# Output transposes by DMA for half of the batches, a merged scaling of k, a third pair buffer and a new schedule model in an attention and mixture-of-experts kernel

## The chip, the cores and the metric

The kernel runs on one core of one Trainium2 chip. The metric is the device time of one execution in microseconds. A program is executed several times; the text gives the median of the runs and, where the scatter matters, every run. Where two kernels are compared by a ratio, it is the mean time of the fast runs of one over the mean of the fast runs of the kernel before that ran in the same rounds on the same chip. It is therefore not quite the ratio of the medians that stand beside it. A ratio comes with its 95% interval.

## The reference

There are two parts, one behind the other. The first is an attention with a feature map ("hedgehog"), without a softmax over positions: 8 batches, 8 heads, 576 positions of 64 numbers. The second is a mixture of 8 experts over the 4608 rows that come out, with a routing table made by 8 rounds of alternate row and column scaling.

```python
def phi(x):                                   # x: batch, head, 576, 64
    proj = einsum('bhsd,df->bhsf', x, w_phi)  # 64 -> 128
    proj = proj - max(abs(proj), axis=-1)
    return concatenate([exp(proj), exp(-proj)], axis=-1)

q_p, k_p = phi(q), phi(k)
kv  = einsum('bhsf,bhsd->bhfd', k_p, v);  z = sum(k_p, axis=2)
x   = einsum('bhsf,bhfd->bhsd', q_p, kv) / (einsum('bhsf,bhf->bhs', q_p, z) + 1e-06)
# x is put into 4608 rows of 512

P = exp(x @ w_gate - max)                     # 4608 x 8
for _ in range(8):                            # routing
    P /= P.sum(1) + 1e-09;  P /= P.sum(0) + 1e-09;  P *= N / E
for e in range(8):
    out += P[:, e] * (relu(x @ w1[e]) @ w2[e])
```

## The kernel before

The work goes through the core as follows.

- **Attention**, to about 212 us. Two heads of a batch make a *pair*; there are 32 of them. For most batches the inputs q and k of two pairs are loaded as 16-bit numbers (tile `qk`) and turned by a DMA transpose on the SyncE queue (`qkT<-qk`, 12 of them, 512 KB each). TensorE multiplies them with `wphi`, VectorE takes maxima (`m`), ScalarE takes exponentials (`k`, `q`, `em`), GpSimd scales v, and the output of a pair (`xb`) is turned again into `xT`, the operand of the experts.
- **Expert 0** is computed plainly. TensorE is not busy with attention alone, so the expert's matmuls fill its gaps. Its weights come in eight pieces (`load_w0`).
- **Routing**, from about 214 to 257 us: a chain of small VectorE operations and one tiny matmul (`cs` by `colw`) in each of 8 rounds, again with expert 0's matmuls as filling.
- **Experts 1 to 7**, each with a scheme of seven products in place of eight, from about 263 us to the end.

Every operation is first recorded with its engine, its estimated duration and its dependencies. A list scheduler then plays the kernel through with those durations and gives each engine a fixed order. The chip executes that order: **each engine does its instructions in the planned sequence, and if the first one must wait, those behind it wait too.** The queue of SyncE goes by its order too: in the kernel before it waited once 14.7 us for GpSimd with a load, and the transfers behind were issued after that, the next of them at 36.7 us. Which operation is preferred is set by the string `order`, each letter of which starts one step of a pair.

```python
class Plan:                                   # parts of schedule()
    ...
    free[o.eng] = at + o.dur
    ...
    if o.nbytes:                              # a DMA: one line for all of them
        dma_free = max(at + o.dur + 1.0, dma_free) + o.nbytes / 1e3
        o.end = dma_free + 1.0
    else:
        o.end = at + o.dur + o.lat
...
def load_w(e, r=()):                          # weights of experts 1 to 7, 2 MB of HBM data in each DMA
    for w, src in ((w1, moe_w1), (w2, moe_w2)):
        dma("POOL", 2 << 20, 280, ... nc.gpsimd.dma_start(out=w(), in_=src[e]...), r, ...)
...
def load_w0(i, r):                            # expert 0: pieces 0-3 are w1, 4-7 are w2
    n = i % 4
    if i < 4:
        dma("POOL", 1 << 19, 250, ... out=w1()[:, :, n * 256:(n + 1) * 256] ..., r, [(w1, n)])
    else:
        dma("POOL", 1 << 19, 280, ... out=w2()[:, 2 * n:2 * n + 2, :] ..., r, [(w2, n)])
...
# pair_a: both signs of k
mk = scores(1, 1)
for y, sg in ((0, -1.0), (1, 1.0)):
    em = s["em"][y]
    exp(10, lambda em=em: em(), lambda: m()[:, 1, :], sg, mk, [em])
    pool(512, lambda ...: nc.gpsimd.tensor_tensor(out=s["v"][y]()[:, :, 0:D], in0=t["v"]()..., in1=em()..., op=ALU.mult), ...)
    pool(4, lambda ...: nc.gpsimd.tensor_copy(out=s["v"][y]()[:, :, D], in_=em()), ...)
...
def pair_c(b, pr, xb):
    if b < 8:                                 # always
        pxt = new("P1")
        for j in range(NJ):
            pe(128, lambda j=j: nc.tensor.transpose(bf(pxt)[:, j * 128:j * 128 + 128], xb()[:, j, :], ident), ...)
        dve(256, lambda: nc.vector.tensor_copy(out=xT[:, pr, b * SM:(b + 1) * SM], in_=bf(pxt)[:, 0:512]), ...)
    else:
        ...                                   # a DMA transpose on the SyncE queue, never taken
...
def stage_a(i):                               # pair i = 4 b + pr
    ...
    gt = [("max", 0, i - 1)] if i >= 1 else []
    if b + 1 < B and pr in (0, 2):            # loads for the next batch
        ...
        load_qk(b + 1, 2 * pr, 4, t, gt); load_v(...); turn_qk(t)
    ...
    n = i - 2
    if 0 <= n < 8:
        load_w0(n, gt)                        # one piece of expert 0 with each pair from the third
...
def sums_x(g):                                # sums of parts of x for the seven products
    X = [new("S") for _ in range(2)]
    for n, y, z, r in (...):
        sub(dve, 512, x(n), y, z, ALU.subtract, xkeys(g) + ["late"] + ..., ...)
    for i in range(2):
        dma("SP", 1 << 18, 250, lambda i=i: nc.sync.dma_start(out=Xd[g][i], in_=X[i]()), ...)
...
if e == 1 and g < 9:                          # the 36 scalings of expert 0's result
    for ts in range(4):
        act(512, lambda ts=ts: nc.scalar.activation(out=acc[g][:, ts, :], in_=acc[g][:, ts, :],
            func=ACT.Copy, bias=0.0, scale=P[:, 4 * g + ts, 0:1]), ["P", ("acc", g, ts)] + akey(g), ...)
...
for e in range(1, E):
    w1, w2 = load_w(e, [("xT", 5, 3)])        # "late" would be: after all of attention
    if e == 1:
        for g in range(NG):
            sums_x(g)
```

## Time and profile before

The kernel before took 1044.54 us (three runs, 1044.49 to 1044.91). In the four later batches of runs its medians were 1044.8 to 1045.0, single runs 1043.5 to 1047.0.

The table by stretches gives, for each stretch of time, the busy time of each engine, the granted clock of TensorE (1.00 is full), the mean number of DMA transfers' packets in work as a share of the engines, and GB/s. These are three of its rows for the kernel before, with the row of column names:

```profile
core 0: us, PE busy (x) PEld busy (x) DVE busy (x) ACT busy (x) POOL busy (x), PEclk, DMA share, GB/s
...
20.00:70.00 50.00, 44.01 (x508) 28.82 (x506) 46.79 (x116) 46.56 (x121) 37.91 (x73) 1.00 1.15 181
...
262.00:300.00 38.00, 35.24 (x304) 29.25 (x303) 26.70 (x47) 37.28 (x74) 10.99 (x9) 1.00 0.34 72
300.00:1040.00 740.00, 739.01 (x6738) 658.93 (x6735) 565.11 (x1008) 458.16 (x958) 314.64 (x250) 1.00 0.27 69
```

TensorE is busy for 739.01 of the 740 us from 300 to 1040 us, so there is no more than about 1 us of gaps to fill there. From 20 to 70 and from 262 to 300 us there is more, 6.0 and 2.8 us. The ends of matmuls are modelled in the profile, so a busy share is a rough number. I therefore also took the step from each matmul's start to the next one's start and compared it with the step of a full stream. For N columns I set that to N/2.4 + 2.5 ns, an estimate: a line through the median steps of this trace, which are 0.056 us between matmuls of 128 columns, 0.109 us for 256 and 0.216 us for 512 (0.160 us more for 384 columns more). What a step takes beyond that is a *stall* if it is over 2.5 times this floor, otherwise it is counted as *slow clock*. The name says more than the trace does: in every stretch of the kernel before the granted clock is 1.00, so for its slow steps a lower clock is not shown. This is a computation of mine from the trace.

Who was waited for from 20 to 70 us shows in the view of waits. Its columns are the engine and line that waited, the operation waited for, and the total, the count and the longest of these waits in us. TensorE in the kernel before:

```profile
engine line waited for: us in total, times, longest us
PE P L407 <- DVE m L399: 2.0, 7, 0.7
PE P L606 <- DVE P L618: 0.8, 2, 0.5
PE P L484 <- DVE m L399: 0.6, 1, 0.6
```

All waits are short ones, and all are for VectorE or ScalarE. No wait for a DMA is in the list. For 255 to 300 us the chain of work that ended last tells what sets the time, in shares of the stretch. Its summary line for the kernel before:

```profile
by line: ACT acc L1181 36.2%; ACT V L1171 13.9%; ACT U L1047 13.8%; issue 8.2%; ACT hT L1056 7.2%; PE P L1019 6.6%; PE P L407 4.4%; DVE hT L1051 3.1%; ACT acc L734 2.1%; DVE acc L1159 1.8%; DVE T L927 1.4%; DVE P L886 1.0%; DVE c_bc L884 0.
```

L1181 is the scaling of expert 0's result, 36 operations on ScalarE. They all become possible at once when the routing ends, and stand in ScalarE's way while it should empty PSUM for expert 1. The groups of instructions that the change touches, up to 345 us (columns: line, engine, operation, tiles and shapes, count | busy us, mean ns of one | idle time before, and for whom):

```profile
L626 DVE TENSOR_TENSOR xb<-P,rec 128x256 bf16<-128x256 f32 x64 | 26.9, 421 | 1.0
...
L1181 ACT ACTIVATE acc<-acc,P 128x512 f32<-128x512 f32 x36 | 25.0, 782 | 0.8 <-DVE P L886 0.8
...
L648 DVE COPY xT<-P 128x512 bf16<-128x512 bf16 x32 | 13.3, 416 | 1.2 <-PE P L645 1.1
...
L645 PE MATMUL P<-ident,xb 128*128 128x128 bf16 x128 | 12.9, 219 | 0.3 <-DVE m L399 0.2
...
L403 ACT ACTIVATE em<-m 128x8 f32<-128x8 f32 x64 | 10.7, 236 | 0.5 <-DVE m L399 0.4
...
L631 DVE TENSOR_TENSOR xb_r<-P,rec 128x128 bf16<-128x128 f32 x32 | 9.0, 281 | 0.0
```

### The profile page before, as it was taken

What the parts mean: (1) busy time and instruction counts of PE and PEld (TensorE: products, weight loads), DVE (VectorE), ACT (ScalarE), POOL (GpSimd) and SP (SyncE); (2) the same over time, 40 slices, a digit from 0 to 9 for tenths busy, and PEclk for the clock granted to TensorE, in tenths of its full rate; (3) what the DMA queues carried; (4) which work ended last, traced back from release to release, by engine and by line L of the source; (5) the groups of instructions that cost most, each with busy time, mean ns of one, the idle gap of its engine ahead of it and who ended that gap; (6) DMA issues with size and microseconds to landing.
All of it is one profiled execution on the core that took longest, in us unless ns stands there. A gap on an engine that the chain in (4) does not pass through costs nothing.

```text
span 1043.5 us, 24529 instructions
## 1 busy us (share of the span) xinstructions
PE 1020.4 (98%) x9512; PEld 842.1 (81%) x9512; DVE 823.9 (79%) x1626; ACT 711.1 (68%) x1570; POOL 461.5 (44%) x532
## 2 busy tenths in 40 slices
PE   6899999999999999999999999999999999999998
PEld 4566666654788888888888888888888888888886
DVE  6999899998777787778877787778777877787775
ACT  7999999944976666666666666565666666666663
POOL 3876757500233344344444444444444443333442
PEclk9999999999999999999999999999999999999999
DMA  9997987734411152113311441134111611114333
GB/s 250 150 196 132 150 127 136 122 122 120 93 41 41 52 105 60 51 42 82 81 41 42 87 87 51 42 69 95 41 42 50 125 51 42 41 43 131 122 122 122
DMA packets 105237, 93.94 MB, mean 90 GB/s; under 512 B 45344, under 2 KB 80288, under 8 KB 105120
## 3 DMA queue, kind: packets, MB, share of 16 engines
q1 hardware_dynamic: 71840, 68.45, 23.6%
q0 software_dynamic: 33120, 23.86, 16.4%
q8 instruction: 74, 1.21, 0.5%
q14 instruction: 43, 0.35, 0.1%
q10 hardware_dynamic: 160, 0.07, 0.0%
HBM read 94.98 MB, written 14.16 MB: 105 GB/s over the span
## 4 chain that ended last, share of the span: by engine, by line
PE 89%; ACT 5%; DVE 3%; DMA 1%; issue 1%; SPq 0%; POOL 0%; DVEq 0%; ACTq 0%
PE P L1019 70%; PE P L407 16%; ACT acc L1181 2%; DVE m L399 1%; PE P L606 1%; ACT k L403 1%; DMA acc<-in_q_dram 1%; DMA wgate_f<-in_moe_w_gate_dram 1%; ACT V L1171 1%; ACT U L1047 1%; PE P L645 1%; DVE xb L626 0%; ACT q L403 0%; DVE P L618 0%; PE P L484 0%
## 5 line engine op out<-in xcount | busy, mean ns | idle before, releaser
L1174 POOL TENSOR_TENSOR acc<-acc,V 128x512 f32<-128x512 f32 x248 | 316.4, 1283 | 440.4 <-ACT V L1171 437.2
L1051 DVE CUSTOM_DVE_ANT_0 hT<-P,U 128x512 bf16<-128x512 f32 x378 | 255.0, 687 | 107.9 <-ACT U L1047 59.7
L1047 ACT COPY U<-P 128x512 f32<-128x512 f32 x378 | 217.8, 590 | 137.4 <-PE P L1019 130.8
L1171 ACT ACTIVATE V<-P,P 128x256 f32<-128x256 f32 x496 | 206.3, 477 | 123.4 <-PE P L1019 121.6
L1159 DVE SCALAR_TENSOR_TENSOR acc<-P,P,acc 128x256 f32<-128x256 f32 x372 | 160.1, 478 | 73.4 <-PE P L1019 71.7
L1019 PEld LDWEIGHTS <-w 128*128 128x128 bf16 x2016 | 197.3, 98 | 23.7 <-issue 0.6
L1019 PEld LDWEIGHTS <-S 128*128 128x128 bf16 x1984 | 194.1, 98 | 23.2 <-issue 0.6
L1019 PEld LDWEIGHTS <-T 128*128 128x128 bf16 x1512 | 147.9, 98 | 19.1 <-issue 2.0
L1019 PEld LDWEIGHTS <-hT 128*128 128x128 bf16 x1488 | 145.4, 98 | 18.3 <-DVE hT L1051 1.1
L1019 PE MATMUL P<-X,w 128*128 128x256 bf16 x1008 | 154.7, 273 | 0.4 <-ACT U L1047 0.4
L1019 PE MATMUL P<-xT,w 128*128 128x256 bf16 x1008 | 152.0, 273 | 0.0
L1019 PE MATMUL P<-X,T 128*128 128x256 bf16 x1008 | 148.6, 273 | 1.3 <-ACT U L1047 1.2
L1019 PE MATMUL P<-w,hT 128*128 128x256 bf16 x992 | 142.6, 273 | 0.6 <-DVE hT L1051 0.6
L1019 PE MATMUL P<-T,S 128*128 128x256 bf16 x1056 | 136.3, 273 | 0.4 <-ACT V L1171 0.4
L1019 PE MATMUL P<-w,S 128*128 128x256 bf16 x928 | 126.6, 273 | 0.0
L532 POOL TENSOR_TENSOR v<-v_m,em 128x512 bf16<-128x512 f32 x64 | 66.8, 1043 | 70.6 <-ACT em L403 57.5
L399 DVE TENSOR_REDUCE m<-P 128x4 f32<-128x512 f32 x128 | 82.7, 681 | 1.7 <-PE P L407 1.2
L1056 ACT ACTIVATE hT<-P 128x512 bf16<-128x512 f32 x126 | 74.6, 607 | 12.9 <-PE P L1019 12.4
L407 PE MATMUL P<-w,hT 128*128 128x512 bf16 x320 | 80.2, 379 | 0.3
L927 DVE TENSOR_TENSOR S<-hT 128x1024 bf16<-128x1024 bf16 x124 | 80.1, 683 | 0.0
L407 PE MATMUL P<-xT,w 128*128 128x512 bf16 x288 | 76.2, 379 | 1.2 <-ACT kr L403 0.5
L1019 PE MATMUL P<-xT,T 128*128 128x256 bf16 x504 | 76.3, 273 | 0.0
(94 smaller groups left out, 1091.7 us busy)
## 6 DMA issues: line engine op xcount, KB each, us to landing
X<-xd SPq DMA_DIRECT2D x126, 256.0 KB, 2.6
w<-in_moe_w_dram POOLq DMA_DIRECT2D x14, 1024.0 KB, 10.4
v_m<-in_v_dram SPq DMA_DIRECT2D x15, 512.0 KB, 5.1
out_dram<-acc SPq DMA_DIRECT2D x14, 512.0 KB, 3.2
xd<-S SPq DMA_DIRECT2D x18, 256.0 KB, 2.0
qk<-in_k_dram POOLq DMA_DIRECT2D x12, 256.0 KB, 5.5
qk<-in_q_dram POOLq DMA_DIRECT2D x12, 256.0 KB, 6.4
w<-in_moe_w_dram POOLq DMA_DIRECT2D x8, 256.0 KB, 7.5
```

What stands on the lines that cost most here:

```text
L399: dve(el, lambda: nc.vector.tensor_reduce(out=dst(), in_=src(), axis=AX.X, op=ALU.max, apply_absolute_value=True), r, w)
L407: nc.tensor.matmul(out_, lhsT=lhsT, rhs=rhs, start=start, stop=stop)
L532: pool(512, lambda y=y, em=em: nc.gpsimd.tensor_tensor(out=s["v"][y]()[:, :, 0:D], in0=t["v"]()[:, h0:h0 + 2].rearrange("p a (b c) -> p (a ...
L927: lambda: f.tensor_tensor(out=out_(), in0=x(), in1=y(), op=op), r, w, **kw)
L1019: pe(256, lambda i=i, k=k, z=z: nc.tensor.matmul(bank()[:, 256 * i:256 * i + 256], lhsT=lhs(k, i), rhs=rhs(k), start=first and z, stop=k = ...
L1047: act(512, lambda: nc.scalar.copy(out=u[fp][n]().rearrange("p a b -> p (a b)"), in_=x[fp]()), [x[fp]], [u[fp][n]])
L1051: dve(500, lambda: nc.vector._custom_dve(ADD_SAT, out=out_(fp, i, j), in0=bank[fp]().rearrange("p (a b) -> p a b", a=2), in1=u[fp][n](), s ...
L1056: act(512, lambda: nc.scalar.activation(out=out_(fp, i, j), in_=x[fp]().rearrange("p (a b) -> p a b", a=2), func=ACT.Relu, bias=0.0, scale ...
L1159: dve(330, lambda n=n, ts=ts: nc.vector.scalar_tensor_tensor(out=acc[g][:, ts, 256 * j:256 * j + 256], in0=bank()[:, 256 * n:256 * n + 256 ...
L1171: act(390, lambda n=n: nc.scalar.activation(out=u()[:, n, :], in_=bank()[:, 256 * n:256 * n + 256], func=ACT.Copy, bias=0.0, scale=P[:, 4 ...
L1174: pool(670, lambda: nc.gpsimd.tensor_tensor(out=acc[g][:, 2 * i:2 * i + 2, 256 * j:256 * j + 256], in0=acc[g][:, 2 * i:2 * i + 2, 256 * j: ...
L1181: act(512, lambda ts=ts: nc.scalar.activation(out=acc[g][:, ts, :], in_=acc[g][:, ts, :], func=ACT.Copy, bias=0.0, scale=P[:, 4 * g + ts, ...
```

## The change

Its intent is to take work off TensorE, VectorE and ScalarE in attention, and to order the rest better:

1. The outputs of batches 3 to 6 (16 pairs) are turned by DMA transposes on the SyncE queue instead of TensorE transposes and VectorE copies.
2. Both signs of the scaling of k are done in one operation: GpSimd writes the negative maxima beside the maxima, one exponential serves both, and one GpSimd multiplication of 1024 elements replaces two of 512.
3. The output of a pair is made in steps of five columns each (with the rest rows inside), so `xb` takes two VectorE operations in place of three.
4. The pair's buffers get a third copy. Its room is taken from the second weight buffer (`wx`), so the weights of expert 1 can't be loaded before attention has ended.
5. The schedule model gets DMA landing times, for which it takes two queues to share the links, a TensorE clock that it can take to be slower, and new speeds and durations. These are assumptions of the model. The order string is new and has finer steps.
6. The 36 scalings wait for the second `hT` of their group, so they spread over expert 1.

The core of the diff:

```diff
@@ schedule model
+class Links:
+    def add(self, o, at):
+        n = int(o.eng == "POOL")
+        self.line[n].append([at + (2.6 if n else 1.65), o.nbytes / 1e3, o])
...
+        share = [1.0, 1.0]
+        if len(on) == 2:
+            share = [0.23, 0.59] if self.line[0][0][2].turn else [0.59, 0.42]
...
-                dma_free = max(at + o.dur + 1.0, dma_free) + o.nbytes / 1e3
-                o.end = dma_free + 1.0
+                links.add(o, at)          # lands at the time of Links, + 0.95
@@ rings
-    ring(wp, [128, 4, FF], BF16, "w1", 2)
-    ring(wp, [128, 8, DD], BF16, "w2", 2)
+    wx = wp.tile([128, 8192], BF16, name="wx")
+    ring(wp, [128, 4, FF], BF16, "w1", 1, 1)      # the second copy is a view of wx
+    ring(wp, [128, 8, DD], BF16, "w2", 1, 1)
-        ring(a_t, [128, 8, DF], BF16, f"k{x}", 2)
+        ring(a_t, [128, 8, DF], BF16, f"k{x}", 2, 1)
...
@@ pair_a
-        for y, sg in ((0, -1.0), (1, 1.0)):
-            em = s["em"][y]
-            exp(10, lambda em=em: em(), lambda: m()[:, 1, :], sg, mk, [em])
-            pool(512, ...)
+        pool(8, lambda: nc.gpsimd.tensor_scalar_mul(m()[:, 1], m()[:, 2], -1.0), mk, [(m, "neg")])
+        exp(16, lambda: em(), lambda: m()[:, 1:3], 1.0, mk + [(m, "neg")], [em])
+        pool(1024, ...)
@@ outs
-            if h == 0:
-                dve(128, lambda: nc.vector.tensor_tensor(out=r["xb"]()[:, pr]..., 
+            dve(320, lambda: nc.vector.tensor_tensor(
+                out=xb()[:, :, 64 * h:64 * h + 64], in0=num()[:, :, 0:D], ...
@@ pair_c
-        if b < 8:
+        if b in (3, 4, 5, 6,):
+            dma("SP", 1 << 17, 148, lambda: nc.sync.dma_start_transpose(
+                out=xT[:, pr, b * SM:(b + 1) * SM]..., in_=xb()[:, 0:NJ]...), ...)
+            return
@@ order
-        "aqraqabbcqabqacbqrbcaqbacuqaqbacqruabgqccucbudbduaqabdqadgrcbucqucabqcauqdua" ...
+        "arqparqbabqbapqnbaqamqmbnpabqpnpbmnpccnrcnpamqcaqpmbupaqumcacrnbqnuanbqampun" ...
@@ scaling of expert 0
-                    scale=P[:, 4 * g + ts, 0:1]), ["P", ("acc", g, ts)] + akey(g),
+                    scale=P[:, 4 * g + ts, 0:1]), ["P", ("acc", g, ts), (hT[1], 0, 1)] + akey(g),
@@ experts
-        w1, w2 = load_w(e, [("xT", 5, 3)])
+        w1, w2 = load_w(e, ["late"])
```

## The prediction

> **What bounds it now.** TensorE. From 300 us on, the table by stretches gives 20.0 busy of every 20 us, with 128x256 matmuls starting 0.109 us apart. [...] I took the step from each matmul's start to the next in TensorE's timeline and compared it with that floor: only 23.6 us are stalls, against about 1,011 us of work; 3.7 us pass before the first matmul and about 6 us after the last. The stalls: 5.1 us before 20 us (start-up, waiting for the first q, k transfers), 11.2 us from 20 to 70, none from 70 to 140, 3.1 us from 140 to 212, none from there to 260, and 4.2 us from 260 to 300. So attention looks bound by ScalarE and VectorE (46.6 and 46.8 busy of 50 us from 20 to 70), but only where TensorE has no expert-0 matmuls to fill with.
>
> **What the change does.**
> - TensorE: 64 output transposes (16 pairs) go to the DMA queue. At 0.055 us a step that is 3.5 us; splitting the rest-row matmuls adds about 0.3. Net -3.2 us, nearly all on the critical path, as it lies in a saturated stretch.
> - VectorE: 16 evictions of 0.416 us go (-6.7 us); the three xb operations of a pair (421+421+281 ns) become two of 320 elements, about 491 ns each by interpolation: -4.5 us in all.
> - ScalarE: 64 em operations of 236 ns and 16 em_r of 227 ns halve: -9.3 us. GpSimd gets a negation per pair, and one 1024-element multiply for two of 1.04 us: a longer chain (about 1 us, an estimate from these) to v, which the third pair buffer should cover.
> - DMA: 16 more transposes of 128 KB on the SyncE queue. The existing ones of 512 KB take 5.3 us to land; DMA engines are 70-90% busy in attention, yet TensorE waited for DMA only at start-up.
> - Expert 1's weights now load after attention (first at 178 us before); landing takes 10-15 us and they are needed at about 257, so no wait.
> - The 36 scalings of acc (782 ns, 25 us of ScalarE between 257 and 300, 36% of that stretch's chain) must now wait for their group's hT, so they spread over expert 1.
>
> **How much shows.** From 70 to 260 savings on ScalarE and VectorE mostly hide. I count: -3.2 TensorE work; 20-70 us: 5% less ScalarE work and better packing, -3.5; 140-212: -1.5; 260-300: -3. Start-up and the rest: nothing, or a little lost to new DMA waits. Together about -11 to -12 us.
>
> **Prediction: 1032.5 us, range 1026.5 to 1039.** Faster by over 2% needs under 1023.6, practically all stalls gone: 4%. Within 2%: 95%. Slower by over 2%: 1%.
>
> **What would show it.** Right: output transposes on TensorE from 128 to 64; steps over the floor fall in 20-70 and 260-300; the first expert-1 matmul comes at about 253 instead of 263; ScalarE and VectorE together lose about 20 us in attention; from 300 us on the stretches stay at 20.0, the last matmul simply earlier. Wrong: TensorE waiting for xT or acc from DMA, for expert-1's w near 250, or for v from GpSimd.
>
> **What would make it wrong.** A late first expert-0 matmul (the new order starts it after nine pairs begun, before after seven)[...]; transposes blocking input loads behind them in the in-order SyncE queue; the longer GpSimd chain. On the other side, the new order may nearly empty 20-70.

Two passages are cut from this text. The first took the floor of a matmul's step from elsewhere and concluded that the part from 300 us on is at it; the floor that the text speaks of after that is the line through measured steps given above. -3.2, -3.5, -1.5 and -3 us come to -11.2 us, the text's -11 to -12.

## The result and the profile after

The changed kernel took 1041.64 us: 1043.33, 1039.95, 1038.93 and 1043.44 (ratio to before 0.997, 0.9951 to 0.9988). A second set of four, run later as a control on another occasion, gave 1040.73, 1042.53, 1036.26 and 1041.74 (0.9955, 0.9926 to 0.9985). It is a little faster, by some 3 to 4 us instead of 11 to 12, and the measured median lies above the upper end of the predicted range. It also scatters over 7 us, where the kernel before scatters over 3.5.

The profiled execution is the one of 1043.33 us. The same three rows of its table by stretches:

```profile
20.00:70.00 50.00, 41.93 (x485) 28.26 (x483) 42.92 (x102) 43.03 (x106) 36.15 (x59) 0.93 1.43 167
...
262.00:300.00 38.00, 38.00 (x332) 32.27 (x330) 27.79 (x48) 29.71 (x59) 10.94 (x9) 1.00 0.41 84
300.00:1040.00 740.00, 737.01 (x6719) 657.15 (x6716) 567.28 (x1004) 468.73 (x980) 314.61 (x250) 1.00 0.27 70
```

The last stretch but one is now full, as hoped. From 20 to 70 us TensorE is busy for 2.1 us less than before, and at a lower granted clock (0.93 instead of 1.00). The accounting of TensorE's steps by stretch, in us, stall + slow clock (differences taken before rounding):

| stretch | before | after | predicted difference | found |
|---|---|---|---|---|
| 0-20 | 5.8 + 2.3 | 2.9 + 2.7 | 0 or a small loss | -2.4 |
| 20-70 | 11.2 + 2.9 | 12.8 + 4.6 | -3.5 | +3.4 |
| 70-140 | 0.0 + 0.7 | 4.2 - 0.2 | 0 | +3.3 |
| 140-212 | 3.1 + 0.9 | 0.4 - 0.2 | -1.5 | -3.7 |
| 212-262 | 0.0 - 0.5 | 2.5 + 1.6 | 0 | +4.6 |
| 262-300 | 4.2 + 0.2 | 0.2 + 0.1 | -3 | -4.1 |
| work at full speed | 1004.2 | 1001.0 | -3.2 | -3.2 |

The gains came, and two of them were larger than predicted: 3.2 + 2.4 + 3.7 + 4.1 = 13.4 us. Against them stand three losses where none, or a gain, was predicted: 3.4 + 3.3 + 4.6 = 11.3 us. That leaves about 2 us, and by so much the last matmul starts earlier (1038.64 before, 1036.70 after).

The groups of instructions that answer to those shown before, up to 345 us, and the chain of 262 to 300 us:

```profile
L1412 ACT ACTIVATE acc<-acc,P 128x512 f32<-128x512 f32 x28 | 20.5, 736 | 0.0
...
L865 DVE TENSOR_TENSOR xb<-ps,rec 128x320 bf16<-128x320 f32 x32 | 15.3, 484 | 0.4
...
L883 DVE COPY xT<-ps 128x512 bf16<-128x512 bf16 x16 | 6.3, 410 | 0.4 <-PE ps L880 0.3
...
L564 ACT ACTIVATE em<-m 128x16 f32<-128x16 f32 x22 | 6.1, 277 | 0.5 <-POOL m L754 0.5
...
L880 PE MATMUL ps<-ident,xb 128*128 128x128 bf16 x40 | 3.9, 228 | 0.1
```

```profile
by line: PE ps L1250 91.0%; PE ps L568 9.7%; issue 0.0%
```

The edits of single operations did what they are meant to. The output copies fell from 32 to 16. The exponential `em` is one of 277 ns instead of two of 236 (22 of the 32 stand here under the tile `em`; the other 10 lie in `wx`, as do some of `xb` and of the transposes). The scalings (L1412, before L1181) are 28 in this window instead of 36, the others come later, and they are out of the chain.

**The loss from 20 to 140 us.** The waits of TensorE in the changed kernel, first from 20 to 70, then from 70 to 140 us:

```profile
PE ps L568 <- DMA qkT<-qk: 3.5, 1, 3.5
PE ps L851 <- DVE m_r L560: 1.0, 1, 1.0
```

```profile
PE ps L568 <- DMA qkT<-qk: 2.0, 2, 1.5
```

TensorE now waits for turned inputs, `qkT`, which it never did before. The chain that ended last, from 20 to 70 us, consists of them for two thirds; the first line is its summary, the others are the two pieces (start, us, what):

```profile
by line: DMA qkT<-qk 68.2%; PE ps L568 9.3%; ACT q L564 5.4%; ACT k L564 3.6%; issue 3.4%; PE ps L698 3.1%; DVE m L560 2.6%; DVE m_r L560 2.6%; ACT wx L564 1.5%; PE ps L851 1.3%; PE ps L624 1.3%; DVE ps L859 1.0%; DVE xb L865 1.0%; DVE rec 
```

```profile
36.81 17.45 DMA qkT<-qk
...
55.98 16.67 DMA qkT<-qk
```

The DMA view has the time from issue to landing. The line is of the transposes issued in the ten microseconds around the first one, once in the kernel before and once in the changed one (KB are not given for a transpose; the last number is us to landing):

```profile
qkT<-qk SPq DMA_TRANSPOSE x1, 5.6
```

```profile
qk<-in_q_dram POOLq DMA_DIRECT2D x1, 256.0 KB, 17.6
...
qkT<-qk SPq DMA_TRANSPOSE x1, 17.4
```

The transpose took 5.6 us to land before and 17.4 us after, as did the other transfers issued beside it: the next q took 17.6 us. The new order itself makes part of this crowd: by 45 us it has issued seven of expert 0's eight weight pieces, the old order three, and the eight land after 7.6 to 19.3 us instead of 4.0 to 8.8 us. TensorE's timeline shows what the wait costs twice over:

```profile
54.30 1.89 PE L568 MATMUL ps<-wphi,qkT 128*128 128x256 bf16 x8 [3.54 <-DMA qkT<-qk]
```

```profile
72.69 1.05 PE L568 MATMUL ps<-wphi,qkT 128*128 128x256 bf16 x8 [0.49 <-DMA qkT<-qk]
```

After a wait of 3.54 us the eight matmuls of 256 columns took 1.89 us, after a wait of 0.49 us 1.05 us. The granted clock (view by stretches) was 0.50 from 52.84 to 59.66 us: it fell while TensorE waited, and the next 5.4 us of matmuls ran at it. From 72.5 to 74 us it was 1.00. How long a wait must be for this is not shown: after the wait of 2.3 us at the routing (below) the clock was 0.50 from 226.92 to 230.33 us, and from 70 to 140 us, with waits for `qkT` of up to 1.5 us, it was 1.00.

How much room each turned input had is best told by its *slack*: TensorE's arrival at the first matmul that needs it, minus the landing. A negative slack is a wait. I computed it from the trace for all 12 transposes; of each, the first three as issue time, us to landing and slack:

| kernel | 1st | 2nd | 3rd | median of 12 | least |
|---|---|---|---|---|---|
| before | 43: 5.6, +5.3 | 61: 10.6, +2.2 | 70: 5.2, +9.5 | +8.7 | +1.3 |
| after | 37: 17.4, -4.0 | 56: 16.7, -0.9 | 72: 8.3, +0.9 | +1.1 | -4.0 |

A late landing is not new: one of the kernel before took 14.3 us, at 184 us, and still had 1.3 us to spare. What is new is that there is no room for one.

**The loss from 212 to 262 us.** The wait of TensorE from 212 to 300 us, and VectorE's longest from 205 to 262:

```profile
PE ps L568 <- DVE cs L1110: 2.3, 1, 2.3
```

```profile
DVE S L1158 <- DMA xd<-S: 2.5, 1, 2.5
```

`cs` is the routing's column sum. Three pieces of the chain that ended last show why it was late:

```profile
215.65 8.14 DMA xd<-S
...
223.81 0.42 DVE S L1158
...
225.84 26.05 PE ps L568 x119
```

VectorE makes the sums of x, which are stored to `xd` from a buffer with few copies. A sum must wait until an older one's store has landed, and the routing's next operation stands behind that sum in VectorE's order. The stores landed late because expert 1's weights, which had been loaded from 178 us on before, now start at 214 us. The stores issued in 205 to 235 us, and the weights beside them:

```profile
xd<-S SPq DMA_DIRECT2D x10, 256.0 KB, 2.1
```

```profile
xd<-S SPq DMA_DIRECT2D x10, 256.0 KB, 7.1
wx<-in_moe_w_dram POOLq DMA_DIRECT2D x2, 1024.0 KB, 14.7
```

### The profile page after: what moved, and what is told of

It reads as the page before. It is cut to its first block, busy times and chain, and to the rows that moved or that the text cites. A ratio compares the mean times of both kernels' runs of the same rounds, so it can differ in the third digit from the quotient of the medians.

```text
span 1041.5 us, 24345 instructions
## 1 busy us (share of the span) xinstructions
PE 1017.8 (98%) x9512; PEld 841.2 (81%) x9512; DVE 821.2 (79%) x1576; ACT 704.9 (68%) x1530; POOL 459.2 (44%) x476
## 4 chain that ended last, share of the span: by engine, by line
PE 91%; DMA 5%; ACT 1%; DVE 1%; POOL 1%; issue 0%; DVEq 0%; SPq 0%; POOLq 0%; ACTq 0%
PE ps L1250 73%; PE ps L568 15%; DMA qkT<-qk 4%; PE ps L851 1%; DMA xd<-S 1%; ACT k L564 1%; ACT q L564 0%; PE ps L698 0%; DMA xT<-xb 0%; DMA acc<-in_k_dram 0%; POOL vrd L678 0%; POOL v L756 0%; DVE S L1158 0%; DVE m L560 0%; DVE m_r L560 0%
## 5 line engine op out<-in xcount | busy, mean ns | idle before, releaser
L1278 ACT COPY U<-ps 128x512 f32<-128x512 f32 x378 | 217.1, 587 | 172.2 <-PE ps L1250 163.0
L1282 DVE CUSTOM_DVE_ANT_0 hT<-ps,U 128x512 bf16<-128x512 f32 x378 | 254.4, 686 | 82.5 <-PE ps L1250 58.0
L1402 ACT ACTIVATE V<-ps,P 128x256 f32<-128x256 f32 x496 | 208.3, 473 | 85.8 <-PE ps L1250 78.9
L1390 DVE SCALAR_TENSOR_TENSOR acc<-ps,P,acc 128x256 f32<-128x256 f32 x372 | 159.7, 477 | 78.9 <-PE ps L1250 78.6
L1250 PE MATMUL ps<-X,T 128*128 128x256 bf16 x1008 | 151.2, 273 | 0.0
L1250 PE MATMUL ps<-T,S 128*128 128x256 bf16 x1056 | 135.8, 273 | 0.1
L1250 PEld LDWEIGHTS <-wx 128*128 128x128 bf16 x1152 | 112.7, 98 | 13.6 <-issue 0.2
L1250 PEld LDWEIGHTS <-w 128*128 128x128 bf16 x864 | 84.5, 98 | 9.8
L1250 PE MATMUL ps<-xT,wx 128*128 128x256 bf16 x576 | 88.7, 273 | 0.0
L1250 PE MATMUL ps<-X,wx 128*128 128x256 bf16 x576 | 86.5, 273 | 0.0
## 6 DMA issues: line engine op xcount, KB each, us to landing
wx<-in_moe_w_dram POOLq DMA_DIRECT2D x8, 1024.0 KB, 10.2
```

What stands on the lines that cost most here:

```text
L1250: pe(256, lambda i=i, k=k, z=z: nc.tensor.matmul(bank()[:, 256 * i:256 * i + 256], lhsT=lhs(k, i), rhs=rhs(k), start=first and z, stop=k = ...
L1278: act(512, lambda: nc.scalar.copy(out=u[fp][n]().rearrange("p a b -> p (a b)"), in_=x[fp]()), [x[fp]], [u[fp][n]])
L1282: dve(515, lambda: nc.vector._custom_dve(ADD_SAT, out=out_(fp, i, j), in0=bank[fp]().rearrange("p (a b) -> p a b", a=2), in1=u[fp][n](), s ...
L1390: dve(320, lambda n=n, ts=ts: nc.vector.scalar_tensor_tensor(out=acc[g][:, ts, 256 * j:256 * j + 256], in0=bank()[:, 256 * n:256 * n + 256 ...
L1402: act(370, lambda n=n: nc.scalar.activation(out=u()[:, n, :], in_=bank()[:, 256 * n:256 * n + 256], func=ACT.Copy, bias=0.0, scale=P[:, 4 ...
```

## The experiments

**Theories.** *D (landing times)*: the new order gives DMA-fed operands hardly any slack; the turned inputs land late because expert 0's weight pieces, the next inputs and the transposes crowd the DMA engines from 30 to 60 us, and that sets the loss from 20 to 140 us. *S (stores)*: the moved load of expert 1's weights delays the stores of the sums, and that sets the loss from 212 to 262 us. *Rivals*: the 16 new output transposes on the SyncE queue hold up the input transposes behind them (T); the longer chain over GpSimd for the scaling of k costs more than it saves (G); the tighter order itself, with any slack, would lose as much elsewhere (E). The recorded expectations use other letters: their A is D, their A2 is S, their B is T. Their C is that the new order asks for the first turned input too early whatever the traffic. Their E is that deeper rings make the input loads the limit; the E of this text is wider. The cold or slow clock of which they speak is the granted clock of 0.50 from 52.84 to 59.66 and from 226.92 to 230.33 us in the changed kernel's trace; half of TensorE's busy time there, 2.7 and 1.7 us, is an estimate of what it cost.

**A measure that helps.** The schedule model holds a planned start for every operation. It is no measurement, but the trace minus the plan, the *lag*, shows exactly where an execution falls behind its own plan. For the profiled execution of the changed kernel ScalarE's lag (VectorE's agrees) is 1.3 us at 50 us, 7.3 at 70, 10.1 at 90, 10.5 at 210, 15.1 at 230 and 15.9 at the end. So nearly all of the time is lost at three places, and these are the waits above. The kernel before can't be read in this way: its own model plans an end some 70 us after the measured one, so that its lag only falls.

### 1. The moved load and the scalings by themselves

Both are edits of the kernel before. The first, the load of the weights after attention:

```diff
-        w1, w2 = load_w(e, [("xT", 5, 3)])
+        w1, w2 = load_w(e, ["late"])
```

> The kernel before with one thing of the change: weights of experts 1 to 7 may load only after attention, so expert 1's two loads issue at about 213 us instead of 178. If theory A2 holds, stores of xd land in 3 us or more in the median instead of 2.0, VectorE and then TensorE wait between 215 and 240, where the kernel before shows none, and it is 1 to 5 us slower (1045.5 to 1049.5). If the load time does not matter there: within 1 us of 1044.5.

Measured: 1043.9 us (before 1044.95 in the same rounds; ratio 0.999, 0.9975 to 1.0005). The expectation failed. The weights took 8.3 and 16.6 us and the first four stores 6.7 to 8.5 us, nearly as in the changed kernel, but VectorE did not wait for them: in the old order the sums stand where there is room. So a late load alone costs nothing. It costs time in an order that has no room for it.

The second, the scalings behind their group's `hT`:

```diff
-                    scale=P[:, 4 * g + ts, 0:1]), ["P", ("acc", g, ts)] + akey(g),
+                    scale=P[:, 4 * g + ts, 0:1]), ["P", ("acc", g, ts), (hT[1], 0, 1)] + akey(g),
```

> The kernel before with one thing of the change: each of the 36 scalings of acc by P for expert 0 waits, in the schedule, for the hT of its group. If these scalings, bunched on ScalarE after 262 us, cause TensorE's 4.2 us of stalls from 260 to 300 (prediction: -3), those stalls fall under 1 us and the kernel takes 1040 to 1041.5 us. If the stalls come from the start of expert 1 itself: still 3 us or more, time unchanged within 1 us.

Measured: 1041.54 us (0.9969, 0.9954 to 0.9984), so 3.4 us for one dependency. The stalls and slow steps from 262 to 300 us fell from 4.4 to 0.9 us. The chain from 255 to 300 us, whose largest part was `acc L1181` with 36.2%, is now:

```profile
by line: PE P L1019 79.0%; PE P L407 18.3%; DVE hT L1051 2.8%; issue 0.2%
```

This one line of the change is worth about what the whole change gained.

### 2. The output transposes by themselves

On the kernel before, half of the outputs turned by DMA, and the same together with the scalings:

```diff
-        if b < 8:
+        if b not in (3, 4, 5, 6):
             pxt = new("P1")
```

> The kernel before with one part of the change: outputs of batches 3 to 6 turned by DMA. My count: 64 transposes of 55 ns off TensorE, so TensorE's work falls by 3.5 us and the time to 1040.5 to 1042.5 if no DMA wait appears. Rival B (the output transposes delay the input transposes on the same in-order queue): landings of qkT after 100 us lengthen, their slack falls under 2 us, TensorE waits for qkT or xT, and the gain is under 1.5 us.

> The kernel before with the two parts that helped it alone: the scalings of acc gated by hT (measured -3.4 us) and outputs of batches 3 to 6 turned by DMA (-1.8 us). If independent: 1039 to 1040.5, with runs within 1.5 us of each other, as the old order has a median of 8 us between a turned input's landing and its use. If they overlap: 1041 to 1042.

Measured: 1043.07 us for the transposes alone (before 1044.86; 0.9983, 0.9968 to 0.9998), and 1041.23 us for both (before 1044.98; 0.9965, 0.995 to 0.998). The expectation for the transposes, 1040.5 to 1042.5 us, was missed by 0.6 us; why they give less than their 3.5 us of TensorE work was not looked into. The single gains of 1.8 and 3.4 us have a sum of 5.2, together they gave 3.75; each of these has an interval of some 1.5 us to either side, so this does not show that they overlap. The 16 transposes of 128 KB landed in 2.4 to 11.7 us, and no input waited for them.

On the changed kernel the outputs go back to TensorE. The model plans anew:

```diff
-        if b in (3, 4, 5, 6,):
+        if b in ():
```

> The changed kernel with all outputs turned on TensorE as in batches 0 to 2. If the output transposes by DMA are the gain that was counted: 2 to 5 us slower than the changed kernel (1043 to 1047), TensorE's work up by 3.5 us. If they are what ate the gain (rival B): faster than the changed kernel, and the waits for qkT between 36 and 100 us gone. Theory D says those waits stay, because the first output transpose is issued at 109 us.

Measured: 1047.89 us (1052.96, 1046.13, 1045.98, 1049.65), about 6 us slower than the changed kernel. Not all of it is TensorE's work: the new plan, from an order string tuned for the old one, ends 6.3 us later in the model already (1031.7 instead of 1025.5 us). The wait for the first turned input is still there, as its waits from 35 to 70 us show:

```profile
PE ps L568 <- DMA qkT<-qk: 4.2, 1, 4.2
```

So rival T falls: the output transposes, the first of which is issued at 109 us, don't cause these waits. What they are worth by themselves is told by the 1.8 us above, not by this newly planned kernel.

### 3. The crowd around the first turned inputs

First with the order of every other engine frozen: the four w2 pieces of expert 0 (first used at 77 us) are moved in GpSimd's queue behind the q load of batch 3.

```diff
-        done = self.schedule()
+        done = [o for o in self.schedule() if o not in self.move]      # move: the four w2 pieces
+        at = done.index(self.mark[3, 0]) + 1                           # mark: q of batch 3
+        done[at:at] = self.move
```

> The changed kernel with the order on TensorE, VectorE and ScalarE kept, but the four loads of expert 0's w2 moved on the GpSimd queue from 39 to 59 us to just behind the q load of batch 3 (57.6 us); they are needed at 77. Theory A (the turned inputs of batches 2 and 3 land late because the weight pieces crowd the DMA engines at that moment): the first turned qkT lands 6 to 10 us after its issue instead of 17.4, TensorE's 3.5 us wait at 51 to 54 falls under 1 us and the cold clock after it (2.6 us) goes; 3 to 6 us faster than the changed kernel, unless the pieces now delay the next turned input and the wait only moves. Rival B (output transposes by DMA are the cost; the first is issued at 109 us): nothing changes at 51 us. Rival C (the new order simply asks for the first turned input too early, whatever the traffic): landing 15 to 17 us after issue, wait stays at 3 to 4 us.

Measured: 1039.91 us (1041.93, 1039.1, 1038.12, 1040.73; before 1044.95; 0.9947, 0.993 to 0.9963). The first transpose still took 15.8 us, not 6 to 10, so the w2 pieces alone are not the crowd. This is what rival C of the expectation had forecast (15 to 17 us), so this run does not decide between C and D; the next one does. The second transpose landed in 8.4 us with 8.2 us to spare. From 20 to 70 us the sum of stalls stayed (14.7 + 2.3 us); part of the wait only moved to ScalarE (1.9 us for `qkT`, 1.9 us for ScalarE). In the median it is 1.7 us better than the first set of the changed kernel and 1.3 us better than the second, within their scatter.

Then all eight pieces cut to an eighth. **The result is wrong**: the rest of the weights is zero.

```diff
-                out=w1()[:, :, n * 256:(n + 1) * 256],
+                out=w1()[:, :, n * 256:n * 256 + 32],
...
-                out=w2()[:, 2 * n:2 * n + 2, :],
+                out=w2()[:, 2 * n:2 * n + 2, 0:64],
...
+    first = [lambda x=x: nc.vector.memset(x(), 0.0) for x in W[0]]     # two fills at the start
```

> Wrong result on purpose: the changed kernel with its eight loads of expert 0's weights cut to an eighth of their bytes (the rest of the tiles zeroed at the start); order on TensorE and ScalarE identical, on VectorE but for two memsets at the start. Set against the start times that the kernel's own schedule plans, TensorE of the changed kernel falls behind by 6.0 us at 50 to 60 us, 3.0 at 70 to 90 and 4.5 at 220 to 230. Theory A (the traffic around them makes turned inputs land late): the first qkT lands under 10 us after its issue instead of 17.4, lag gained between 40 and 100 us is under 2.5 us instead of 9, and the kernel takes 1031 to 1036 us with the lag at 220 to 230 kept. Rival (transposes next to the q and k loads alone are as slow): landing over 14 us, lag of 5 us or more, 1038 or more.

Measured: 1038.83 us (1037.81 to 1039.18; before 1044.98; 0.9941, 0.9926 to 0.9956). The first transpose lands in 7.1 us instead of 17.4, the second in 4.3, and the waits for `qkT` from 20 to 70 us are gone. The line of the DMA view (38 to 50 us), and the largest waits of TensorE from 20 to 70 us:

```profile
qkT<-qk SPq DMA_TRANSPOSE x1, 7.1
```

```profile
PE ps L851 <- DVE m_r L560: 1.0, 1, 1.0
PE ps L568 <- DVE m L560: 0.7, 3, 0.3
```

ScalarE's lag grows by 0.6 us from 40 to 100 us, against 9.1 in the changed kernel, and the scatter of the four runs falls to 1.4 us. This is the plainest support of D, and it rules out C: the traffic of the weights is what makes the transposes late. The second transpose shows it best, 4.3 us here and 15.0 to 17.4 in all five executions of section 7. The lag shows it less well, for one of those five grew by only 1.4 us with all the traffic. The expected time of 1031 to 1036 us was missed. The total gains less than the lag would let one hope, because the two fills at the start cost about 3 us (the same four `q` operations of ScalarE start at 36.2 us in its chain, at 33.0 us in that of the changed kernel) and the loss after 212 us stays (about 3 us of ScalarE's lag from 220 to 230).

A version with right results keeps all the data and only moves pieces in GpSimd's queue: piece 1 of w1 behind the rest rows of batch 2, pieces 2 and 3 behind a q load of batch 2, w2 behind the first q of batch 3.

```diff
+        for behind, moved in ((("r", 2), self.w0[1:2]), ((2, 4), self.w0[2:4]),
+                              ((3, 0), self.w0[4:8])):
+            done = [o for o in done if o not in moved]
+            at = done.index(self.mark[behind]) + 1
+            done[at:at] = moved
```

> The changed kernel with identical order on TensorE, VectorE and ScalarE and all its bytes, only the GpSimd queue reordered: piece 1 of expert 0's w1 behind the rests' loads of batches 2 to 4, pieces 2 and 3 behind the second q load of batch 2, the four w2 pieces behind the first q load of batch 3, each still ahead of its use in the plan. Theory A: first qkT lands in 7 to 12 us, TensorE's wait for it is under 1 us, 1034 to 1039. If lateness only moves to the weight pieces: new waits for w between 45 and 75 us and no gain against 1041.

Measured: 1041.15 us (1042.12, 1039.95, 1047.1, 1040.17; 0.9977, 0.9942 to 1.0012). The first transpose lands in 10.9 us with 3.0 us to spare, and TensorE waits for no `qkT` before 70 us. But it waits more for ScalarE (1.6 us) and VectorE, and the total is that of the changed kernel, not the expected 1034 to 1039 us. Here the reordering did not make the crowd smaller; it chose who waits.

### 4. Giving the plan slack

The model is told that each transpose lands 4 us later than it thought; everything is planned anew. The second kernel has the edit of section 5 as well.

```diff
-                o.end = landed[0] + 0.95
+                o.end = landed[0] + 0.95 + (4 if o.turn else 0)
```

> The changed kernel with one number of its schedule model altered: a DMA transpose is taken to land 4 us later than the model has it, so the static order asks for turned inputs later. Theory D (the new order asks for each turned input about 1 us after it lands, median 1.1 us against 8.7 before, so every late landing stalls TensorE, and the time differs from execution to execution): median slack 4 us or more, TensorE's waits for qkT between 36 and 100 us fall from 5.5 us to under 1.5 us, the spread of runs falls from 4.5 us to under 2.5 us, and the median is 1034 to 1039. Rival E (deeper rings make the input loads themselves the limit, whatever the order asks): the same waits reappear elsewhere, 1040 or more.

> As the run before, and the sums of x for groups 2 to 8 of expert 1 are made after P is known, so that VectorE's routing chain does not stand behind a store of xd while expert 1's weights load at about 214 us. If that store wait costs what the changed kernel's profile shows (2.5 us of stall and 1.6 us of slow clock between 212 and 262), both go and it is 2.5 to 4 us faster than the run with slack alone. If the stall there is TensorE's order only, it stays at 2 us or more. If the later sums now crowd VectorE in expert 1, stalls appear after 262.

Measured: 1045.55 us (1045.78, 1049.71, 1043.13, 1045.33; 1.0009, 0.9983 to 1.0035) and 1043.95 us (0.9988, 0.9971 to 1.0004). In the first kernel the median slack is 4.5 us, the waits for `qkT` before 140 us are gone and the lag at 100 us is 3.2 us instead of 10.2; in the second one such wait, of 2.4 us, stays. But the plan itself has become 10 us longer, probably because the order string was tuned for the old one. So rival E is right about the time of this edit: the margin cost at least as much as the waits it removed. The recorded E, loads as the limit, is not what was seen, since the loss is in the plan. Whether a new search of the order with the margin in it would do better was not tried. D's expectation failed in two points: the time (1034 to 1039 us) and the scatter, which is 6.6 us although the waits for `qkT` had gone. So those waits are not the only source of scatter.

### 5. The stores beside expert 1's weights

First the load of expert 1 cut to a half (w1) and a quarter (w2), order unchanged. **The result is wrong.**

```diff
+                return t[:, 2:4] if w is w1 else t[:, 6:8]      # for e == 1
...
-                out=w(), in_=src[e].rearrange("(c p) f -> p c f", p=128)),
+                out=part(w()), in_=part(src[e].rearrange("(c p) f -> p c f", p=128))),
```

> Wrong result on purpose: the changed kernel with the two loads of expert 1's weights cut to a half and a quarter of their bytes, same instruction order. Theory A2 (these loads, now issued at 214 us, slow the stores of xd, VectorE waits 2.5 us for a store at 221, the routing chain and TensorE behind it wait 2.3 us and the clock drops): the wait of VectorE for xd at 221 falls under 0.7 us, TensorE loses under 1 us between 212 and 262 against about 4.2 (2.5 of stall, 1.7 of slow clock), and the kernel is 3 to 4 us faster than the changed one. Rival (VectorE is simply slower there than the order assumed): TensorE's wait for the routing sum stays at 2 us or more.

Measured: 1039.31 us (1034.17, 1037.93, 1041.04, 1040.7; 0.9938, 0.991 to 0.9967). In the profiled run the first four stores land in 5.2 to 7.0 us (8.1 to 9.4 in the changed kernel) and the later ones in 2.0 to 4.1, VectorE waits 1.4 us for them instead of 2.5, and stall and slow clock from 212 to 262 us are 1.6 us instead of 4.1. That is the direction of S, but short of what was expected (under 0.7 us and under 1 us). By its lag that run was also 6.5 us better before 212 us, where nothing had been changed: its first transpose took 10.9 us and not 17.4. The landing of the same transfer in the same program differs that much between executions, and a good part of the scatter comes from there (section 7).

Then the stores are moved out of the load's way, with right results: the sums of the groups from 2 on wait for the end of the routing. Until 212 us every engine's order is unchanged. The control, the changed kernel unaltered, ran on the same chip.

```diff
-                xkeys(g) + ["late"] + [(X[i // 2], i % 2) for i in r]
+                xkeys(g) + ["late"] + (["P"] if g >= 2 else []) + [(X[i // 2], i % 2) for i in r]
```

> The changed kernel again, unaltered, as the control of this batch: its four runs so far went from 1038.9 to 1043.4 us. Theory (landing times of the crowded DMA at 36-56 us differ from execution to execution): again a spread of 3 us or more, median 1039-1043.5, and the wait for the first turned q, k at about 51-54 us between 0 and 4 us in the profiled run, the wait for the routing's cs about 2.3 us. Rival (the first profile was an outlier): spread under 1.5 us and no wait for turned inputs.

> Changed kernel, sums of x of groups 2 to 8 only after the routing; every engine's order before 212 us is as it was. Theory (the stores of the sums, landing in 8-9 us among expert 1's weights, hold VectorE and the routing behind it, and TensorE 2.3 us plus a slow clock): wait for cs 0 to 0.5, total 2 to 4 us under the control's median of this batch. Rival (routing is late for another reason, or the lost time returns where expert 1's sums now bunch up): within 1 us of the control.

Measured: control 1041.23 us (1040.73, 1042.53, 1036.26, 1041.74), with the edit 1040.63 us (1040.7, 1040.56, 1035.82, 1041.94; ratios 0.9955 and 0.9951). The waits for `cs` from 212 to 300 us, the control first:

```profile
PE ps L568 <- DVE cs L1110: 1.7, 1, 1.7
```

```profile
PE ps L568 <- DVE cs L1110: 0.2, 1, 0.2
```

The wait is gone, as S says, but the gain is not the 2 to 4 us expected of it: 0.6 us in the medians, within the scatter, as the rival said. Two things explain it. The control's own wait was 1.7 us, while the first profile's was 2.3 us, with the granted clock at 0.50 for 3.4 us after it (whether the control's wait lowered the clock is not shown here). And a new wait took its place. Without the sums in between, the routing's rounds follow each other in 3.4 us, and TensorE meets each of the eight `cs` matmuls 0.1 to 0.4 us too early, 2.0 us in all. In the first profile these small waits were 0.3 us. By TensorE's steps the loss from 212 to 262 us is thus 4.1 us in the first profile, about 2.6 in the control and 2.0 with the edit. (The last two traces lack some matmul records, so these are sums of the steps at the `cs` matmuls and of the slow ones.) S holds as the cause, but taking it away gave back only 0.6 to 2.1 us.

### 6. Both edits together, and the scaling of k

The edit of section 5 together with each reordering of section 3:

> Changed kernel with both edits: the w2 pieces of expert 0 behind the q load of batch 3 in the GpSimd queue, order otherwise frozen, and the sums of x after the routing. If the two losses are separate they add: the first alone measured 1039.9 us, the second is thought worth 2 to 4, so 1036 to 1038, the fastest of all. If they overlap: 1038.5 or more.

> As the run before, plus the sums of x of groups 2 to 8 after P, so that stores of xd (8 to 9 us to landing while expert 1's weights load, against 2.0 to 2.5 in the kernel before) no longer stand in the way of the routing chain. TensorE's wait for the routing sum at 220 goes (2.3 us to under 0.5) and the run is 2 to 4 us faster than the reordered queue alone: 1031 to 1036, the best so far. If nothing is gained, the routing chain itself, now in one piece, is what TensorE waits for.

Measured: with the w2 pieces moved 1039.39 us (1037.89 to 1039.6; 0.9945, 0.993 to 0.9959); with all pieces moved **1038.13 us** (1038.59, 1038.08, 1038.18, 1036.76; before 1044.98; 0.9933, 0.9919 to 0.9948). Both are slower than their expectations for losses that add (1036 to 1038 and 1031 to 1036 us). The second has the lowest ratio of the right versions (the kernel below has a lower median, but runs from 1034.67 to 1045.57 us). Its mean of 1037.9 us lies 3.0 us under the mean of all eight runs of the changed kernel (1040.9), and its scatter is 1.8 us against 7.2. But it is the best of several tries, it ran in an earlier batch than the control, and the intervals of the two ratios overlap, so a part of the 3 us may be luck. In both kernels the waits for `cs` are down to 0.2 us.

The last run undoes the merged exponential alone. The order stays frozen; in place of the negation and the exponential of 16 columns stand two exponentials of 8 (the one multiplication of 1024 elements stays):

```diff
-        pool(8, lambda: nc.gpsimd.tensor_scalar_mul(m()[:, 1], m()[:, 2], -1.0), mk, [(m, "neg")])
-        exp(16, lambda: em(), lambda: m()[:, 1:3], 1.0, mk + [(m, "neg")], [em])
+        pool(8, lambda: None, mk, [(m, "neg")])
+        def both():
+            for y, sg in ((0, -1.0), (1, 1.0)):
+                nc.scalar.activation(out=em()[:, y], in_=m()[:, 2], func=ACT.Exp, scale=sg)
+        act(16, both, mk + [(m, "neg")], [em])
```

> Changed kernel with the order of every engine frozen, only the merged scaling of the pairs undone: two exponentials of 8 columns in place of the GpSimd negation and one exponential of 16. If merging is worth what its ScalarE time says (32 x about 0.2 us, of which only the part before 70 us, about 10 pairs, can show): up to 2 us slower than the control. If the longer chain through GpSimd cost something: 0 to 2 us faster. I expect within 1.5 us of the control.

Measured: 1037.24 us (1037.36, 1037.12, 1034.67, 1045.57; 0.9945, 0.9896 to 0.9994). The median is 4 us under the control's, the scatter is 11 us, and the interval covers the control's ratio. Its profiled run was ahead of the control's by 5.0 us of lag at 210 us; its third transpose, for one, landed after 8.2 us, the control's after 11.2. So merging the exponentials brought nothing that could be seen, and rival G, that its longer chain costs something, is not excluded.

### 7. One order, five executions

Up to 212 us five of the profiled kernels (the changed one, its control, and three whose edits leave the order there alone) are the same order. Their lag behind the plan in us (VectorE's), and their time:

| execution | first transpose lands after | lag at 60 us | at 100 us | at 210 us | at the end | time of this run | time minus last lag |
|---|---|---|---|---|---|---|---|
| changed kernel | 17.4 | 6.9 | 10.2 | 10.5 | 15.9 | 1043.33 | 1027.4 |
| control a_same | 11.8 | 1.8 | 8.3 | 9.7 | 13.3 | 1040.73 | 1027.4 |
| a_sx | 14.8 | 5.4 | 8.0 | 9.9 | 13.2 | 1040.70 | 1027.5 |
| a_twofix | 11.5 | 1.6 | 3.7 | 4.7 | 9.9 | 1037.36 | 1027.5 |
| a_cute1 | 10.9 | 2.0 | 3.0 | 4.0 | 6.7 | 1034.17 | 1027.5 |

The last column is the same for all by construction: the lag at the end is the end minus the planned end, and the plan is the same. What tells more is the lag at 300 us, which is 15.7, 13.1, 13.1, 9.9 and 6.5 us in the order of the table, within 0.2 us of the lag at the end. A microsecond lost before is thus not regained later, when TensorE is full. Between 40 and 100 us one and the same order loses from 1.4 us (a_cute1) to 9.3 (the changed kernel's profile), by when the transposes happen to land. In the control the large wait was not at 51 but at 75 us, 3.5 us again, for a transpose that took 11.2 us.

## Why the prediction was wrong

The step that failed is the overlap of transfers with work. The prediction let the DMA of the inputs and of expert 1's weights run beside the engines at no cost, and forecast -3.5 us for 20 to 70 us and nothing for 70 to 140 and 212 to 262. The runs showed waits for landings there, of turned inputs and of stores, and +3.4, +3.3 and +4.6 us in the profiled execution.

Point by point, as the prediction put it:

- *"Net -3.2 us"* of TensorE work: right, 1004.2 to 1001.0 us. The TensorE transposes of outputs went from 128 to 64. Undoing it cost some 6 us (a_noturn, whose new plan is itself 6.3 us longer), doing it alone on the kernel before gave 1.8.
- *"260-300: -3"*: right in mechanism, small in size. It was 4.1 us in the changed kernel and 3.4 us alone (b_gate).
- *"140-212: -1.5"*: too small. Stall and slow clock there fell from 4.0 to 0.2 us in the first profile.
- *"20-70 us: 5% less ScalarE work and better packing, -3.5"*: wrong, and this is the first of the steps that failed. ScalarE and VectorE had been the limit of that stretch; after the change the limit was the landing of turned inputs. It lost 3.4 us in the profile, and 70 to 140 us another 3.3. The packing itself was not far off: in the execution of a_cute1, which waited for no `qkT` before 70 us, stalls and slow clock from 20 to 70 us were 9.3 + 2.5, so 2.3 us less than in the kernel before.
- *"DMA engines are 70-90% busy in attention, yet TensorE waited for DMA only at start-up"*: true of the kernel before (7 to 9 tenths busy in the slices of its profile to 209 us) and the reason for the mistake. It was read as "DMA has room". In fact the old order had room for DMA: a slack of 8.7 us in the median, which the new order spent. "Not waited for" says nothing of how much is left.
- *"Expert 1's weights now load after attention ... so no wait"*: right for the weights, wrong for what they run beside. The weights took 10.2 and 19.1 us; the stores beside them took 8 to 9 instead of 2. A VectorE sum waited for a store, the routing stood behind it, and TensorE behind the routing: a term set at nothing that was 4.6 us in the profile and about 3 in the control (2.6 against the -0.5 of the kernel before).
- *"Start-up and the rest: nothing"*: start-up gained 2.4 us.
- *"ScalarE and VectorE together lose about 20 us in attention"*: too large. Over the whole span ScalarE lost 6.2 us and VectorE 2.7; up to 212 us it was 4.1 and 3.4. The output transposes, the merged scaling and the wider `xb` did what they were costed for by group, but other operations got slower, such as the sums of `hT` (683 to 720 ns each).
- *"transposes blocking input loads"* was named as a danger and did not come. *"TensorE waiting for xT or acc from DMA"* was the sign to look for, but the wait was for `qkT`, the inputs. The prediction looked at the transfers that the change adds, not at those that it leaves alone and gives less time. A late first expert-0 matmul, named too, came by 1.8 us (41.2 instead of 39.4 us), but a_cute1, where it came at 41.8 us, still lost less from 20 to 70 us than the kernel before. The first expert-1 matmul, forecast at about 253 us instead of 263, started at 265.3 us (263.2 before).

What the sum would have been without the three losses, the prediction had nearly right: the gains were 13.4 us by the accounting, and a run without any lag would have taken about 1027.5 us. The terms that it missed were on the side of the costs. The new schedule model computes one landing time for each transfer and plans closely with it; a landing much later than that is then a wait: for the first transpose, after 17.4 us, it was 3.5 us.

Not settled: the merged exponential could not be told from the scatter, the merged multiplication was not isolated, and the third buffer of the pairs was not isolated, since without it the plan is a different one. Why the same transfer lands after 10.9 us in one execution and after 17.4 in another stays open too; only that it lands after 7.1 us without the weights' traffic is shown, in one execution (a_cutw0).

## What to carry to other kernels

Before a fixed order is tightened, list for each operand that a DMA brings how long before its use it lands; an operand that "is never waited for" may have 9 us to spare or none, and a plan made with one landing time for each transfer can use that room up, as it did here. (A transpose of 512 KB landed after 4.2 us at the least in the kernel before and after up to 17.4 us in the changed one, a store of 256 KB after 2.0 us at the least and after up to 9.4 us beside expert 1's weights.) When a load is moved in time, look at which transfers run there already and what stands behind them in an in-order engine, not only at when the load itself is needed. And where a plan exists, subtract it from the trace: the few places at which the difference jumps are the whole loss.
